# One place per weight chunk, and one region for early and late attention buffers, in a kernel of attention, low-rank mixing and a feed-forward

## The chip, the cores and the metric

The kernel runs on one core of a Trainium2 chip. The metric is the time of one execution on the device, in microseconds (us); of several executions the median is taken. Inside the core, TensorE (PE in the profile) multiplies matrices into PSUM, VectorE (DVE), ScalarE (ACT) and GpSimd (POOL) work on tiles, and SyncE (SP) issues the transfers between HBM and SBUF, all on one queue, in order.

## The reference

The inputs are `q`, `k`, `v` of 8 batches x 8 heads x 576 positions x 64, and the weights `U` (576x32), `V` (32x576), `w_ch1` (512x2048), `w_ch2` (2048x512). Cut to what matters:

```python
q_d, k_d, v_d = means of 4 neighbouring positions of q, k, v      # 144 positions
out_up    = repeat(softmax(q_d @ k_d.T / 8) @ v_d, 4)             # global part
out_local = softmax(where(|i - j| < 4, q @ k.T / 8, -1e9)) @ v    # band of 7 keys
x  = (out_up + out_local), heads side by side                     # 8 x 576 x 512
u  = x + (x.T @ U @ V).T                                          # mixing over positions
out = u + relu(u @ w_ch1) @ w_ch2                                 # feed-forward
```

The weights arrive in 64-bit floats.

## The kernel before

**Work.** Attention goes by head pairs: 4 pairs per batch, 32 in all, numbered here from 0. Pairs 0 to 3 (batch 0, "early", line 939) keep everything on the chip: `early_global`, `local_blocks`, `early_mix`. Pairs 4 and up ("late", line 951) go through DRAM: `late_global` stores the scores `s_s` and the global result `up_s`, `local_attn` reads them back (`sc`, `ul`), forms the products `Pt` on POOL (L800), sums them on DVE (L805) and stores `x_s`, and `mix_part` reads `x_s`, multiplies with `U` (`Ust`, L849) and `V` (`Vst`, L864), and leaves the feed-forward's input `u` as a high part `uH` and a rest `uL`. The early mixing does the same with L675, L677 and L692 to L695.

The feed-forward goes by steps (batch, half of 288 positions, chunk `fc` of 128 hidden units): 16 x 16 = 256 steps, 32 to a batch. `ffn1` (L889) does 12 matmuls into `ps_h`, ACT makes `hH` (L897), DVE `hL` (L898), and three steps later `ffn2` (L913) does 12 matmuls into the four banks `acc0` to `acc3`. A batch's first step needs `uH` and `uL` of all four pairs of that batch.

**Weights.** Each of the 32 chunks (16 of W1, 16 of W2) is loaded as raw 64-bit words, 512 KB, and converted (`convert`): ACT L343, DVE L345, L347, L349 with an intermediate `y` in a PSUM bank, ACT L354 writes the high part, POOL L357 the rest. W1 goes into two big tiles `W1H` and `W1L`. The raw words of W1, of the first three W2 chunks and of `U` pass through a ring of three buffers that they share with the late pairs' products:

```python
def raw_buf(name):
    return buf(loc, [128, 2 * CN], I32, name, "Pt:raw", 3)
```

The other W2 chunks have a place each, into which the raw words are loaded too. These places (`w2p`) lie where the early pairs' buffers were, so nothing is written to them before the early pairs are done: that point is an operation that the code calls `late` (line 961). The raw words of `Ub` (another layout of `U`) and of the two halves of `V` pass one after the other through one buffer (`eraw`).

**PSUM.** The banks are `acc0` to `acc3`, `h0`, `h1` and a ring of two, `m`. A conversion's `y` lies in `acc2` and `acc3` in turn for W1, in `h1` for W2 and `U`. The first `ffn2` waits until all 16 W1 chunks have their high part, since it takes these banks.

**Order.** The program is written out ahead of time by a planner (`Plan.run`): every operation has an engine, an estimated duration and a priority (smaller goes first). The planner simulates the five queues with these estimates, and each engine then executes its list in that order. On the chip an instruction that must wait holds back all behind it on its engine; SP's transfers too. Priorities: pair n has 10 n to 10 n + 2, W1 chunk f has 20 + 2 f, W2 chunk f has 20 + f, `U` 38, a feed-forward matmul over 1000 (so PE takes it when nothing of attention is ready), its relu -10.

Of the kernel before, what the change touches and what calls it, by code (L numbers as in the profile page):

```python
# [51 lines left out]
class Plan:  # L52
# [147 lines left out]
def attn_mix_ffn_kernel(ctx: ExitStack, tc, q, kp, vp, qT, kT, v, U, Ub, V, w1, w2, mask, band, eye, ex, pool, vw, vn, ident, outT):  # L200
# [15 lines left out]
    LAG = 3  # L216
    W1S, W2P, W2S = 2, 20, 1
    W1A, AT, W1B, W1C = 5, 25, 1.6, 15
# [3 lines left out]
    pw = lambda prio: PW0 if prio < 10 else PWx  # L222
    W1P = 20
    W2D = 4
    H1 = NFC + LAG
# [13 lines left out]
    const = ctx.enter_context(tc.tile_pool(name="const", bufs=1))  # L239
    loc = ctx.enter_context(tc.tile_pool(name="loc", bufs=1))  # L240
    glo = ctx.enter_context(tc.tile_pool(name="glo", bufs=1))
    mix = ctx.enter_context(tc.tile_pool(name="mix", bufs=1))
    ffn = ctx.enter_context(tc.tile_pool(name="ffn", bufs=1))
# [26 lines left out]

    mask_sb = const.tile([128, NPOS, 7], F32, name="mask_sb")
    warm = const.tile([128, 1], F32, name="warm")
# [4 lines left out]
    Vst = const.tile([128, S], F32R, name="Vst")  # L277
    W1H = const.tile([128, NDC, DF], F32R, name="W1H")
    W1L = const.tile([128, NDC, DF], F32R, name="W1L")
    early = tc.tile_pool(name="early", bufs=1)  # L280
    early_pool = early.__enter__()

    class Late:
        pool = None

        def open(self):
            early.__exit__(None, None, None)
            self.pool = ctx.enter_context(tc.tile_pool(name="w2p", bufs=1))

        def tile(self, *args, **kw):  # L290
            return self.pool.tile(*args, **kw)

    w2p = Late()

# [37 lines left out]
    def convert(raw, pp, n, hi_out, lo_out, a, wkey, name, prio, gate=(), l0=0):  # L332
# [18 lines left out]
        own = lambda k: [wkey + k] if isinstance(wkey, str) else [(wkey, k)]  # L351
        if gate:
            done.append(plan.ops[-1])
        act(n, lambda: nc.scalar.activation(hi_out(), ta(), AF.Copy), [t, *gate], own("H"), prio)  # L354
        if lo_out is None:
# [4 lines left out]

    def early_raw(name):
        return buf(early_pool, [128, S], I32, name, "eraw", 1)

    def raw_buf(name):
        return buf(loc, [128, 2 * CN], I32, name, "Pt:raw", 3)

    def load_ublk(prio):
        raw = early_raw("ur")
# [3 lines left out]
        pu = psum(ps_m, "ps_p", "m:p", 2)  # L372
        u4 = lambda: pu()[:QH, :2 * R].rearrange("p (a r) -> p a r", a=2)
# [8 lines left out]
    def load_u(prio):  # L382
        raw = raw_buf("ur")
        dma(lambda raw=raw: nc.sync.dma_start(out=raw()[:MP, :2 * MJ * R], in_=U.bitcast(I32)),
            [], [raw], prio, 150)
        convert(raw, MP, MJ * R, lambda: Ust[:, :, 0:R], lambda: Ust[:, :, R:2 * R], MJ, "U", "cu", prio)

    def load_v(prio):
        hs = S // 2
        for c in range(2):  # L390
            raw = early_raw("vraw")

            dma(lambda raw=raw, c=c: nc.sync.dma_start(
                out=raw()[:, :2 * hs], in_=V.bitcast(I32)[:, c * S:(c + 1) * S]), [], [raw], prio)
            cs = slice(c * hs, (c + 1) * hs)
            convert(raw, 128, hs, lambda cs=cs: Vst[:, cs].unsqueeze(1),
                    lambda cs=cs: Vst[3 * R:4 * R, cs].unsqueeze(1), 1, f"V{c}", "cv", prio, l0=3 * R)

    def load_w1(f, prio):
        raw = raw_buf("w1r")  # L400
        dma(lambda: nc.sync.dma_start(
            out=raw(), in_=w1.bitcast(I32)[f],
        ), [], [raw], min(prio - W1A, W1B + W1C * f if f < 3 else prio), 525)
        fs = slice(f * 128, (f + 1) * 128)
        convert(raw, 128, CN, lambda: W1H[:, :, fs], lambda: W1L[:, :, fs], NDC, f"W1_{f}", "c1", prio)

    W2 = [buf(w2p, [128, 2, DM], F32R, f"W2_{f}", f"W2_{f}:w") for f in range(NFC)]

    done = []

    def load_w2(f, prio):
        ahead = f < 3
        raw = raw_buf("w2r") if ahead else buf(w2p, [128, 2 * CN], I32, "w2r", f"W2_{f}:raw")
        dma(lambda: nc.sync.dma_start(out=raw(), in_=w2.bitcast(I32)[f * 128:(f + 1) * 128, :]),
            [] if ahead else ["late"], [raw], prio, 525, after=done[f - W2D:f - W2D + 1] if f >= W2D else ())
        convert(raw, 128, CN, lambda: W2[f]()[:, 0:1, :], lambda: W2[f]()[:, 1:2, :], 1, W2[f], "c2", prio, ["late"])

# [345 lines left out]
    def local_attn(b, hp, up_s, x_s, s_s, prio):  # L763
# [6 lines left out]
        sb = ex = ms  # L770
        dve(63, lambda: nc.vector.scalar_tensor_tensor(ms(), sc(), 0.125, mask_sb, op0=ALU.mult, op1=ALU.add),  # L771
            [sc, "mask"], [ms], prio)
        dve(63, lambda: nc.vector.tensor_reduce(out=mx(), in_=ms(), axis=AX.X, op=ALU.max), [ms], [mx], prio)
# [105 lines left out]
    def ffn1(s, i):  # L879
        b, t, fc = s  # L880
        uH, uL = u_of(b, t)
        ps = psum(ps_h, "ps_h", f"h{i % 2 * (i >= H1):d}:f", 1)
        fs = slice(fc * 128, (fc + 1) * 128)

        def mm():
            n = 0
            for dc in range(NDC):
                for w, u in ((W1H, uH), (W1H, uL), (W1L, uH)):
                    nc.tensor.matmul(ps()[:, :TN], w[:, dc, fs], u()[:, dc, :],  # L889
                                     start=(n == 0), stop=(n == 3 * NDC - 1))  # L890
                    n += 1
        ur = [(uH, c) for c in range(NDC)] + [(uL, c) for c in range(NDC)]
        mm_op[i] = op(PE, PH, mm, ur + [f"W1_{fc}H", f"W1_{fc}L"] + ["late"] * (i >= 3), [ps], FILL + i,
                      [mm_op[i - 1]] if i >= H1 else ())
# [7 lines left out]
    def ffn2(s, i):  # L902
# [6 lines left out]
        for e in range(NDC):  # L909
            def mm(e=e):  # L910
                es = slice(e * 128, (e + 1) * 128)
                for n, (w, hx) in enumerate(((0, hH), (0, hL), (1, hH))):
                    nc.tensor.matmul(ac[e]()[:, :TN], W2[fc]()[:, w, es], hx(),  # L913
                                     start=(fc == 0 and n == 0), stop=(fc == NFC - 1 and n == 2))
            first = [f"W1_{f}H" for f in range(NFC)] * (i == 0)
            op(PE, PF, mm, [hH, hL, (W2[fc], "H"), (W2[fc], "L")] + first, [ac[e]], FILL + i + LAG - 0.5)
        if fc == NFC - 1:
            uH, uL = u_of(b, t)
            for e in range(NDC):
                if e == NDC - 1:  # L920
                    o1 = buf(loc, [128, TN], F32, "o1", "o1b", 1)
                else:
# [118 lines left out]
```

## Time and profile before

| | |
|---|---|
| three runs | 1035.8, 1030.01, 1033.21 us; median 1033.21 |
| profiled execution | 1031.25 us, of which the trace spans 1029.4 us |
| PE, DVE, ACT, POOL busy | 990.8, 504.4, 390.2, 550.6 us |
| mean granted clock of TensorE | 0.983 |
| HBM read, written | 87.89 MB, 30.86 MB |

"Busy" of PE counts a matmul from its start to its modelled end, and pipelined matmuls overlap. In the views below a line number is that of the kernel's code, "out<-in" are the names of its tiles, and times in a list are us from the start of the span.

### The profile page before, as it was taken

The page shows a single profiled execution, that of the slowest core. Times are in us where ns is not written, and L with a number is a line of the kernel's source. Part 1 is how long each engine was busy: PE and PEld are TensorE (multiplying, and loading weights), DVE is VectorE, ACT ScalarE, POOL GpSimd, SP SyncE. Part 2 cuts the span into 40 slices and gives each one's busy share as a digit, 9 for nine tenths or more (in the row PEclk, how much of TensorE's full clock was granted, in tenths as well). Part 3 has the DMA queues.
Part 4 walks back from the last instruction along what each step waited for, and adds up shares of the span by engine and source line. Part 5 has one row for each costly group of instructions (what it writes and reads, how often), then busy time and mean ns, then how long its engine had stood idle before and what let it go on. Part 6 is the DMA issues. An engine that isn't in the chain of part 4 may idle for free.

```text
span 1029.4 us, 26839 instructions
## 1 busy us (share of the span) xinstructions
PE 990.8 (96%) x10792; PEld 972.9 (95%) x10792; DVE 504.4 (49%) x1022; ACT 390.2 (38%) x1239; POOL 550.6 (53%) x580
## 2 busy tenths in 40 slices
PE   5888979989999999999999999999999999999998
PEld 4677979989999999999999999999999999999998
DVE  4778986544454447544454545445654424212111
ACT  3667643433334334443343442334443232111110
POOL 3545895783756656685665756457575605211010
PEclk8899999989999999999999999999999999999999
DMA  9748854573454546555544453556555231000000
GB/s 291 200 136 237 256 132 123 133 154 98 103 142 105 142 118 148 121 120 144 121 126 115 122 122 83 122 134 156 126 135 129 78 76 35 24 1 24 1 24 24
DMA packets 222452, 120.51 MB, mean 117 GB/s; under 512 B 174756, under 2 KB 198136, under 8 KB 222328
## 3 DMA queue, kind: packets, MB, share of 16 engines
q1 hardware_dynamic: 222328, 118.79, 46.0%
q8 instruction: 85, 1.39, 0.6%
q14 instruction: 39, 0.32, 0.1%
HBM read 87.89 MB, written 30.86 MB: 115 GB/s over the span
## 4 chain that ended last, share of the span: by engine, by line
PE 90%; DVE 3%; ACT 2%; DMA 2%; issue 1%; SPq 1%; POOL 0%; DVEq 0%; ACTq 0%
PE acc L913 38%; PE ps_h L889 38%; PE ps_a L563 3%; PE ps_b L720 2%; PE ps_hu L849 2%; PE ps_t L550 1%; PE ps_b L727 1%; PE ps_u L864 1%; PE ps_v L445 1%; DMA w2r<-in_W 1%; DVE ms L771 1%; DMA ul<-up_s 1%; PE ps_u L695 1%; DMA pool_sb<-in_pool 0%; PE ps_hu L675 0%
## 5 line engine op out<-in xcount | busy, mean ns | idle before, releaser
L913 PE MATMUL acc<-hH,W 128*128 128x288 f32 x2048 | 464.0, 299 | 0.1
L913 PEld LDWEIGHTS acc<-hH,W 128*128 128x128 f32 x2048 | 344.8, 188 | 1.6 <-POOL W L357 0.5
L889 PE MATMUL ps_h<-uH,W1H 128*128 128x288 f32 x1024 | 305.9, 299 | 11.1 <-DVE hL L898 11.1
L889 PE MATMUL ps_h<-uL,W1H 128*128 128x288 f32 x1024 | 304.2, 297 | 0.0
L898 DVE SCALAR_TENSOR_TENSOR hL<-ps_h,hH 128x288 fp32r<-128x288 f32 x256 | 116.7, 456 | 382.4 <-ACT hH L897 381.6
L889 PE MATMUL ps_h<-uH,W1L 128*128 128x288 f32 x1024 | 302.9, 296 | 0.0
L913 PE MATMUL acc<-hL,W 128*128 128x288 f32 x1024 | 301.9, 295 | 0.0
L800 POOL TENSOR_TENSOR Pt<-vl,at 128x896 f32<-128x896 f32 (+1 forms) x140 | 241.9, 1806 | 90.3 <-DVE acc L805 40.2
L897 ACT ACTIVATE hH<-ps_h 128x288 fp32r<-128x288 f32 x256 | 105.1, 411 | 432.1 <-PE ps_h L889 431.8
L889 PEld LDWEIGHTS ps_h<-uH,W1H 128*128 128x128 f32 x1024 | 194.3, 190 | 12.9 <-DVE hL L898 12.6
L889 PEld LDWEIGHTS ps_h<-uH,W1L 128*128 128x128 f32 x1024 | 194.7, 190 | 0.0
L889 PEld LDWEIGHTS ps_h<-uL,W1H 128*128 128x128 f32 x1024 | 194.4, 190 | 0.0
L913 PEld LDWEIGHTS acc<-hL,W 128*128 128x128 f32 x1024 | 192.7, 188 | 0.0
L805 DVE TENSOR_REDUCE acc<-Pt 128x128 f32<-128x1024 f32 (+1 forms) x140 | 151.1, 1105 | 6.7 <-ACT Pt L794 2.4
L841 POOL TENSOR_TENSOR xL<-xL,xH 116x640 fp32r<-116x640 f32 x28 | 44.0, 1572 | 96.5 <-ACT xH L840 83.5
L872 POOL TENSOR_TENSOR uL<-xT,uH 128x288 fp32r<-128x288 f32 x56 | 44.3, 816 | 84.5 <-ACT uH L870 84.4
L924 POOL TENSOR_TENSOR o<-uH,uL 128x288 f32<-128x288 f32 x64 | 49.8, 817 | 53.0 <-DMA out_t<-o 53.0
L521 POOL TENSOR_TENSOR vr<-vr 72x256 f32<-72x256 f32 x56 | 41.6, 743 | 41.7 <-DMA vr<-in_v 37.0
L745 ACT ACTIVATE se<-ps_b 96x114 f32<-96x114 f32 x112 | 40.0, 357 | 59.3 <-PE ps_b L720 37.8
L794 ACT ACTIVATE Pt<-ul 128x128 f32<-128x128 f32 (+1 forms) x140 | 50.3, 444 | 18.7 <-DVE acc L805 14.5
L536 ACT ACTIVATE E<-ps_b,nb 72x144 f32<-72x144 f32 x112 | 40.9, 372 | 0.6
L531 DVE TENSOR_REDUCE mx<-ps_b 72x2 f32<-72x288 f32 x56 | 23.4, 449 | 27.6 <-ACT se L745 27.6
(137 smaller groups left out, 986.4 us busy)
## 6 DMA issues: line engine op xcount, KB each, us to landing
vl<-in_vp SPq DMA_DIRECT2D x56, 240.0 KB
out_t<-o SPq DMA_DIRECT2D x64, 144.0 KB
w1r<-in_W SPq DMA_DIRECT2D x16, 512.0 KB
w2r<-in_W SPq DMA_DIRECT2D x16, 512.0 KB
gT<-in_kT SPq DMA_DIRECT2D x28, 291.0 KB
gq<-in_qT SPq DMA_DIRECT2D x28, 288.0 KB
vr<-in_v SPq DMA_DIRECT2D x56, 144.0 KB
up_s<-od SPq DMA_DIRECT2D x112, 72.0 KB
```

Of the source, the lines that this page charges most:

```text
L521: pool_tt(256, lambda x=x: nc.gpsimd.tensor_tensor(out=x()[:, :, 0:2, :], in0=x()[:, :, 0:2, :], in1=x()[:, :, 2:4, :], op=ALU.add), [x], ...
L536: act(SD, lambda a=a, hh=hh, nb=nb: nc.scalar.activation(Es[hh]()[:, a, :], pooled_view(ps[hh])[:, a], AF.Exp, bias=nb()[:, a:a + 1], scal ...
L794: act(n * D, lambda n=n, ps=ps, Pt=Pt: nc.scalar.activation(Pt()[:, :n, :, 7], ul()[:, ps, :], AF.Copy), [ul], [(Pt, 1)], prio, 0.16)
L800: nc.gpsimd.tensor_tensor(out=Pt()[:, :n, :, 0:7].rearrange("p s d o -> p o s d"), in0=win, in1=at()[:, ps, :].rearrange("p s o -> p o s") ...
L805: dve(8.5 * n * D, lambda n=n, ps=ps, Pt=Pt: nc.vector.tensor_reduce(out=acc()[:, ps, :], in_=Pt()[:, :n], axis=AX.X, op=ALU.add), [(Pt, 0 ...
L841: pool_tt(640, lambda: nc.gpsimd.tensor_tensor(out=xL(), in0=xL().bitcast(F32), in1=xH().bitcast(F32), op=ALU.subtract), [xL, xH], [xL], prio)
L872: pool_tt(TN, lambda uH=uH, uL=uL, uf=uf: nc.gpsimd.tensor_tensor(out=uL()[:, hp, :], in0=uf(), in1=uH()[:, hp, :].bitcast(F32), op=ALU.su ...
L889: nc.tensor.matmul(ps()[:, :TN], w[:, dc, fs], u()[:, dc, :], start=(n == 0), stop=(n == 3 * NDC - 1))
L897: last_h[i] = act(TN, lambda: nc.scalar.activation(hH(), ps()[:, :TN], AF.Relu), [ps], [hH], FIRST, 0.05)
L898: dve(TN, lambda: nc.vector.scalar_tensor_tensor(hL(), ps()[:, :TN], 0.0, hH().bitcast(F32), op0=ALU.max, op1=ALU.subtract), [ps, hH], [hL ...
L913: nc.tensor.matmul(ac[e]()[:, :TN], W2[fc]()[:, w, es], hx(), start=(fc == 0 and n == 0), stop=(fc == NFC - 1 and n == 2))
L924: pool_tt(TN, lambda e=e, o1=o1: nc.gpsimd.tensor_tensor(out=o1()[:, :TN], in0=uH()[:, e, :].bitcast(F32), in1=uL()[:, e, :].bitcast(F32), ...
```

## The change

Each of the 32 weight chunks gets a place of its own (`wts`), for both parts, and its raw words are loaded into the same place; there is no ring for raw words any more. `Ub`, the two halves of `V` and `U` are loaded through the places of W2 chunks 15, 14, 13 and 12. The late pairs' three pools (`loc`, `glo`, `mix`) now lie where the early pairs' buffers were, and every operation that uses them comes after `late` (the `gate`). The conversions are in one list in order of use: W1 0 to 3, then W1 and W2 in turn, with priorities 30 to 45; a load is planned at the earliest when the conversion four places ahead of it is done. From the 13th conversion on `y` lies in `h1`, and the first `ffn2` waits for the first 12 chunks of the list. The early mixing's PSUM goes from the ring `m` to `acc0` and `acc1`. `U` has priority 36; the mask's load comes after `late`.

```diff
+        deps.update(d for k in (*r, *w) for d in getattr(getattr(k[0] if isinstance(k, tuple) else k, "pool", None), "gate", ()))
...
-    W1S, W2P, W2S = 2, 20, 1
+    W1F, WS = 4, 0.4
...
-    W1P = 20
-    W2D = 4
+    W1P = 30
+    WD = 4
+    NA = 12
...
-    W1H = const.tile([128, NDC, DF], F32R, name="W1H")
-    W1L = const.tile([128, NDC, DF], F32R, name="W1L")
...
+    loc, glo, mix = (Late(n) for n in ("loc", "glo", "mix"))
+
+    def open_late():
+        early.__exit__(None, None, None)
+        for p in (loc, glo, mix):
+            p.open()
...
-    dma(lambda: nc.sync.dma_start(out=mask_sb, in_=mask), [], ["mask"], 35, 32)
...
-        if gate or name == "cu" and lo_out is not None:
+        if own_bank:
             y = buf(ps_h, [128, CN], I32, "y_h", "h1:" + name, 1)
...
-    def early_raw(name):
-        return buf(early_pool, [128, S], I32, name, "eraw", 1)
-
-    def raw_buf(name):
-        return buf(loc, [128, 2 * CN], I32, name, "Pt:raw", 3)
+    def raw_in(f, name):
+        return buf(wts, [128, 2 * CN], I32, name, f"W2_{f}:{name}")
...
-            raw = early_raw("vraw")
+            raw = raw_in(NFC - 2 - c, "vraw")
...
+    W1 = [buf(wts, [128, 2, NDC, 128], F32R, f"W1_{f}", f"W1_{f}:w") for f in range(NFC)]
+    W2 = [buf(wts, [128, 2, DM], F32R, f"W2_{f}", f"W2_{f}:w") for f in range(NFC)]
+    weights, done = [], []
+
+    def load_w(w, src, hi, lo, a, prio, dprio):
+        weights.append(w)
+        raw = buf(wts, [128, 2 * CN], I32, "wr", w.tag + ":raw")
+        dma(lambda: nc.sync.dma_start(out=raw(), in_=src), [], [raw], dprio, 525,
+            after=done[len(done) - WD:len(done) - WD + 1] if len(done) >= WD else ())
+        convert(raw, 128, CN, hi, lo, a, w, "c" + w.tag[1], prio, len(done) >= NA)
...
-        ph = psum(ps_m, "ps_hu", "m:x", 2)
+        ph = psum(ps_acc, "ps_hu", "acc0:x", 1)
...
-            pu = psum(ps_m, "ps_u", "m:x", 2)
+            pu = psum(ps_acc, "ps_u", f"acc{1 - t}:x", 1)
...
-                for w, u in ((W1H, uH), (W1H, uL), (W1L, uH)):
-                    nc.tensor.matmul(ps()[:, :TN], w[:, dc, fs], u()[:, dc, :],
+                for w, u in ((0, uH), (0, uL), (1, uH)):
+                    nc.tensor.matmul(ps()[:, :TN], W1[fc]()[:, w, dc, :], u()[:, dc, :],
...
-            first = [f"W1_{f}H" for f in range(NFC)] * (i == 0)
+            first = [(w, "H") for w in weights[:NA]] * (i == 0)
...
-    for f in range(NFC):
-        load_w1(f, W1P + W1S * f)
-    plan.op(DVE, 0.0, w2p.open, [], ["late"], 27, after=early_ops, lat=0.0)
-    for f in range(NFC):
-        load_w2(f, W2P + W2S * f)
-    load_u(38)
+    for c in range(NFC + W1F):
+        if c < NFC:
+            load_w1(c, W1P + WS * (2 * c - min(c, W1F)))
+        if c >= W1F:
+            load_w2(c - W1F, W1P + WS * (2 * c + 1 - W1F))
+    late = plan.op(DVE, 0.0, open_late, [], [], 27, after=early_ops, lat=0.0)
+    for p in (loc, glo, mix):
+        p.gate.append(late)
+    load_u(36)
+    mask_sb = buf(loc, [128, NPOS, 7], F32, "mask")
+    dma(lambda: nc.sync.dma_start(out=mask_sb(), in_=mask), [], [mask_sb], 40, 32)
```

More of the change, by code (lines that the diff above doesn't have):

```diff
@@ L283, in attn_mix_ffn_kernel, with __init__ @@
     class Late:
-        pool = None
+        def __init__(self, name):
+            self.name, self.pool, self.gate = name, None, []
         def open(self):
-            early.__exit__(None, None, None)
-            self.pool = ctx.enter_context(tc.tile_pool(name="w2p", bufs=1))
+            self.pool = ctx.enter_context(tc.tile_pool(name=self.name, bufs=1))
         def tile(self, *args, **kw):
             return self.pool.tile(*args, **kw)
-    w2p = Late()
+    loc, glo, mix = (Late(n) for n in ("loc", "glo", "mix"))
[3 more added lines that the diff above has]
+            p.open()
     band_sb = early_pool.tile([128, NS * KL], BF16, name="band_sb")
@@ L351, in convert @@
         own = lambda k: [wkey + k] if isinstance(wkey, str) else [(wkey, k)]
-        if gate:
+        if not isinstance(wkey, str):
             done.append(plan.ops[-1])
-        act(n, lambda: nc.scalar.activation(hi_out(), ta(), AF.Copy), [t, *gate], own("H"), prio)
+        act(n, lambda: nc.scalar.activation(hi_out(), ta(), AF.Copy), [t], own("H"), prio)
         if lo_out is None:
@@ L359, in convert @@
             [t, *own("H")], own("L"), prio)
-    def early_raw(name):
-        return buf(early_pool, [128, S], I32, name, "eraw", 1)
-    def raw_buf(name):
-        return buf(loc, [128, 2 * CN], I32, name, "Pt:raw", 3)
+    def raw_in(f, name):
+        return buf(wts, [128, 2 * CN], I32, name, f"W2_{f}:{name}")
     def load_ublk(prio):
-        raw = early_raw("ur")
+        raw = raw_in(NFC - 1, "ubr")
         dma(lambda raw=raw: nc.sync.dma_start(
@@ L371, in load_ublk @@
         convert(raw, 128, NS * R, lambda: Ublk[:, :, 0:R], None, NS, "Ub", "cu", prio)
-        pu = psum(ps_m, "ps_p", "m:p", 2)
+        pu = psum(ps_acc, "ps_p", "acc1:p", 1)
         u4 = lambda: pu()[:QH, :2 * R].rearrange("p (a r) -> p a r", a=2)
@@ L382, in load_u @@
     def load_u(prio):
-        raw = raw_buf("ur")
+        raw = raw_in(NFC - 4, "ur")
         dma(lambda raw=raw: nc.sync.dma_start(out=raw()[:MP, :2 * MJ * R], in_=U.bitcast(I32)),
             [], [raw], prio, 150)
-        convert(raw, MP, MJ * R, lambda: Ust[:, :, 0:R], lambda: Ust[:, :, R:2 * R], MJ, "U", "cu", prio)
+        convert(raw, MP, MJ * R, lambda: Ust[:, :, 0:R], lambda: Ust[:, :, R:2 * R], MJ, "U", "cu", prio, True)
     def load_v(prio):
@@ L397, in load_v @@
                     lambda cs=cs: Vst[3 * R:4 * R, cs].unsqueeze(1), 1, f"V{c}", "cv", prio, l0=3 * R)
-    def load_w1(f, prio):
[L400 to L409, printed above, removed]
-    def load_w2(f, prio):
[L412 to L416, printed above, removed]
+    W1 = [buf(wts, [128, 2, NDC, 128], F32R, f"W1_{f}", f"W1_{f}:w") for f in range(NFC)]
[7 more added lines that the diff above has]
+        convert(raw, 128, CN, hi, lo, a, w, "c" + w.tag[1], prio, len(done) >= NA)
+    def load_w1(f, prio):
+        load_w(W1[f], w1.bitcast(I32)[f], lambda: W1[f]()[:, 0], lambda: W1[f]()[:, 1], NDC, prio,
+               min(prio - W1A, W1B + W1C * f if f < 3 else prio))
+    def load_w2(f, prio):
+        load_w(W2[f], w2.bitcast(I32)[f * 128:(f + 1) * 128, :], lambda: W2[f]()[:, 0:1, :],
+               lambda: W2[f]()[:, 1:2, :], 1, prio, prio)
     def work(is_early, pool, shape, dt, name, tag=None, bufs=1):
@@ L770, in local_attn @@
         sb = ex = ms
-        dve(63, lambda: nc.vector.scalar_tensor_tensor(ms(), sc(), 0.125, mask_sb, op0=ALU.mult, op1=ALU.add),
-            [sc, "mask"], [ms], prio)
+        dve(63, lambda: nc.vector.scalar_tensor_tensor(ms(), sc(), 0.125, mask_sb(), op0=ALU.mult, op1=ALU.add),
+            [sc, mask_sb], [ms], prio)
         dve(63, lambda: nc.vector.tensor_reduce(out=mx(), in_=ms(), axis=AX.X, op=ALU.max), [ms], [mx], prio)
@@ L882, in ffn1 @@
         ps = psum(ps_h, "ps_h", f"h{i % 2 * (i >= H1):d}:f", 1)
-        fs = slice(fc * 128, (fc + 1) * 128)
         def mm():
@@ L892, in ffn1 @@
         ur = [(uH, c) for c in range(NDC)] + [(uL, c) for c in range(NDC)]
-        mm_op[i] = op(PE, PH, mm, ur + [f"W1_{fc}H", f"W1_{fc}L"] + ["late"] * (i >= 3), [ps], FILL + i,
+        mm_op[i] = op(PE, PH, mm, ur + [(W1[fc], "H"), (W1[fc], "L")], [ps], FILL + i,
                       [mm_op[i - 1]] if i >= H1 else ())
@@ L920, in ffn2 @@
                 if e == NDC - 1:
-                    o1 = buf(loc, [128, TN], F32, "o1", "o1b", 1)
+                    o1 = buf(ffn, [128, TN], F32, "o1", "o1b", 1)
                 else:
```

7 lines of the change are left out of this document (2 added, 5 removed).

## The prediction

> **What bounds the kernel now.** I read the 40 slices first, then busy time by stretches, then the chain that ended last, then who waits on the SP queue and on DVE.
>
> ```profile
> PE   5888979989999999999999999999999999999998
> PEclk8899999989999999999999999999999999999999
> ```
>
> ```profile
> 0.00:77.00 77.00, 55.87 (x950) 47.67 (x951) 48.29 (x109) 43.23 (x130) 36.52 (x56) 0.89 0.69 210
> 77.00:225.00 148.00, 134.00 (x1547) 130.15 (x1546) 108.18 (x202) 77.77 (x234) 107.84 (x107) 0.94 0.67 175
> 225.00:1029.40 804.40, 800.91 (x8299) 795.06 (x8298) 347.96 (x711) 269.23 (x876) 406.25 (x417) 1.00 0.41 98
> ```
>
> The columns are: stretch, length, busy time of PE, weight loads, DVE, ACT, POOL, then the granted clock, DMA share and GB/s. From 225 us on PE is idle for 804.40 - 800.91 = 3.5 us at full clock: nothing is left to win there, and whatever moves the beginning moves the end by as much. So the change is decided before 225 us. In the stretch of 77 to 225 us PE loses 148.00 - 134.00 = 14.0 us to idling and 134.00 x 0.06 = 8.0 us to a low clock, 22.0 in all. What separates the stages is in the chain:
>
> ```profile
> 51.75 0.47 DVE cv L349
> 52.24 0.44 ACT Vst L354
> ...
> 77.34 1.64 PE ps_h L889 x12
> ...
> 219.06 0.82 PE ps_u L864 x2
> 219.88 5.61 PE ps_h L889 x24
> ```
>
> At 77.3 the feed-forward of batch 0 starts: the end of the early pairs, which I call E. At 219.1 pair 7's last mixing product comes, and batch 1's feed-forward follows at once. So the attention of batch 1 (pairs 4 to 7) is what ends last before the saturated part. The feed-forward is only just ahead of it:
>
> ```profile
> 215.93 0.46 PE L849 MATMUL ps_hu<-xL,Ust 116*64 116x128 f32 x5
> 219.06 0.82 PE L864 MATMUL ps_u<-Vst,stk 128*128 128x288 f32 x2 [2.67 <-DVE stk L854]
> ```
>
> PE has nothing but pair 7 to do from about 216 on. To gain much, both must come earlier: batch 0's feed-forward and the attention of pairs 4 to 7.
>
> **Raw words in their own places.** No instruction is added: 32 loads and 32 conversions stay, 12 matmuls a step too. The tiles keep 128x128 weights and 128x512 writes, so each instruction costs what it did: 0, with nothing to cover. What goes is the wait for the ring:
>
> ```profile
> SPq L401 <- DVE c L349: 28.5, 12, 4.3
> ```
>
> SP stood 28.5 us for raw buffers, and with it everything queued behind. Those buffers came free at DVE's pace, so the first question is what DVE could have done:
>
> ```profile
> 8.00:36.00 28.00, 20.00 (x417) 16.98 (x418) 13.92 (x36) 14.01 (x51) 9.50 (x14) 0.88 0.85 274
> 36.00:77.00 41.00, 34.31 (x462) 29.61 (x461) 29.83 (x63) 27.53 (x78) 22.12 (x25) 0.88 0.58 172
> L347 DVE SCALAR_TENSOR_TENSOR y_a<-w1r,y_a 128x512 int32<-128x512 int32 x13 | 9.0, 692 | 0.3
> L345 DVE TENSOR_SCALAR y_a<-c 128x512 int32<-128x512 int32 x13 | 8.9, 686 | 2.1 <-ACT c L343 1.8
> L349 DVE SCALAR_TENSOR_TENSOR c<-w1r,y_a 128x512 int32<-128x512 int32 x13 | 8.8, 679 | 0.2
> ```
>
> One chunk takes DVE 0.69 + 0.69 + 0.68 = 2.06 us; 13 chunks are done by E, 19 are left for the attention of batch 1 to share DVE with. From 8 to 36 us DVE idles 14.1 us: room for 6 chunks. Bounds: 0 chunks (the waits were for transfers and for early results) to 6 more by E. I take 3, the middle, because DVE's idle is scattered between the early pairs' own results. That leaves 3 x 2.06 = **6.2 us** less on DVE in the way of pairs 4 to 7 (0 to 12.4). From the 13th conversion on the intermediate has one bank instead of two, for four chunks of W1 that had two. DVE works through a chunk in sequence anyway; what it could lose is the idle before L345, 2.1 / 13 = 0.16 us, once more for each: 0 to 0.6 us, and I take 0.
>
> **V in places of its own.** Before, the second half of V waits for the first's buffer:
>
> ```profile
> 15.52 0.33 SPq L393 DMA_DIRECT2D vraw<-in_V  x1
> ...
> 36.18 0.37 SPq L393 DMA_DIRECT2D vraw<-in_V  x1
> ```
>
> It is issued 20.7 us after the first, and `Vst` is complete at 52.7, on the chain above; all eight early mixing products stand behind it. After, both halves can be loaded before 20 us, and the mixing of pairs 0 and 1 moves into PE's gaps. PE bounds what that can bring: in 36 to 77 us it idles 6.7 us and loses 34.31 x 0.12 = 4.1 to the clock, 10.8 together. I take E **5 us** earlier, at 72.3 (0 to 10.8), about half, since PE's own work stays the same and only its gaps can be filled. Weight conversions also now rank behind pairs 0 to 2; that is in the 5. The mixing's PSUM moves to `acc0` and `acc1`, which the local scores use: these are a few short holds, so 0, at worst 2 us back.
>
> **The shared region.** Now nothing of pair 4 may be loaded before E. Its loads go out at E, and the nearest rows for the way from there to its scores are pair 0's:
>
> ```profile
> 1.65 0.43 SPq L580 DMA_DIRECT2D qt<-in_qT  x1
> ...
> 4.67 0.67 POOL L429 TENSOR_TENSOR gh<-qt 128x288 f32<-128x288 f32 x1 [1.39 <-DMA qt<-in_qT]
> ...
> 6.54 0.43 POOL L431 TENSOR_TENSOR smk<-gh 128x144 f32<-128x144 f32 x1
> ```
>
> From issue to the pooled key 6.97 - 1.65 = 5.3 us. Before, that was done at 35 to 54 us, beside other work, and the scores came right after E:
>
> ```profile
> 35.00 0.60 SPq L580 DMA_DIRECT2D gq<-in_qT  x1
> ...
> 78.91 0.33 PE L727 MATMUL ps_b<-smk,smq 64*32 64x144 f32 x6
> ```
>
> After: 72.3 + 5.3 = 77.6 against 78.9, so **1.3 us** earlier. With E unmoved it would be 82.6, 3.7 later; with E at 66.5, 7.1 earlier. The wait now sits on SP: weight loads are queued behind it, but 15 chunks or so are then in place. The mask moves behind E too, one issue of 0.4 us; its first reader comes 14.8 us after pair 4's scores, so 0. `U` is converted earlier; pair 4's mixing, which needs it, comes tens of us later: 0.
>
> **What holds DVE at 145 us.** The largest loss of the middle stretch is one instruction:
>
> ```profile
> 145.00:160.00 15.00, 9.16 (x64) 8.92 (x63) 12.24 (x16) 5.91 (x24) 8.71 (x13) 0.77 0.41 105
> 145.45 6.20 DVE ms L771
> L771 DVE SCALAR_TENSOR_TENSOR ms<-sc,mask_sb x28: 209/218/6281, 93.7 to 849.4; 128x63 f32<-128x63 f32 x28
> 145.02 2.33 POOL L924 TENSOR_TENSOR o<-uH,uL 128x288 f32<-128x288 f32 x3
> ...
> 151.12 0.44 POOL L523 TENSOR_TENSOR vs<-vr 72x128 f32<-72x128 f32 x1
> PE ps_h L889 <- DVE hL L898: 11.1, 7, 5.8
> ```
>
> Its median is 0.22 us; once it takes 6.28, just while POOL runs without a gap from 145.02 to 151.56. The relu's DVE half stands behind it, and PE behind that, for 5.8 us at the longest. In the new order it need not meet such a run, but POOL has as much to do (107.84 of 148 us): I take half of 6.28 - 0.22 = 6.1, **3.0 us** (0 to 6.1). The Trainium skill, SBUF — State Buffer, section "Who interferes with whom", says that a DVE instruction with two SBUF inputs, as this one has, is shut out by a GpSimd instruction that reads SBUF, for the whole of it. The rows agree; by that rule alone the block is no late load and would come back wherever POOL is backlogged, and the sum would be 1024. Had it been a late load, which the new order moves, it would go whole, and the sum would be 1018.
>
> **The start of the feed-forward.** From 77 to 100 us PE loses a little as well:
>
> ```profile
> 77.00:100.00 23.00, 19.12 (x311) 17.73 (x310) 18.46 (x38) 17.83 (x53) 11.65 (x13) 0.93 0.82 246
> L354 ACT ACTIVATE W<-c x16: 615/628/682, 89.1 to 140.7; 128x512 fp32r<-128x512 f32 x16
> ```
>
> PE idles 3.9 us here and loses 1.3 us to the clock. `ffn2` waits for the high part of 16 chunks of W1 and for its own of W2, the first of which is written at 89.1; after, it waits for 12 chunks in order of use, which by the count above are done by E. I take 4 of these 5.2 us. With E's 5, and half of what PE loses from 145 to 160 us (5.8 idle and 9.16 x 0.23 = 2.1 of clock), batch 0's feed-forward ends 5 + 4 + 4 = 13 us earlier, near 203. That is more than the attention gains below, so PE waits for pair 7 again, some us longer than now, and this part is not in the sum.
>
> **Sum.** Attention of batch 1: 1.3 + 6.2 + 3.0 = 10.5 us earlier, at 208.6, and the saturated part with it. Against the profiled execution's own 1031.25: 1031.25 - 10.5 = **1021**. That execution is 1.96 us (0.2%) below the median of the three runs, inside their spread; I add nothing.
>
> **Rivals.**
> PE as the bound: pairs 4 to 7 keep up and PE loses nothing between E and the saturated part. That gives 5 + 22.0 = 27 us, **1004**. For it: pairs 4 to 7 leave DVE and POOL idle for 40 of 148 us each. Against: four pairs must then be done 16 us sooner than I reckon.
> Nothing comes of it: V and the ring were hidden behind PE's own early work, E stays, pair 4 starts 3.7 later, and the chunks converted ahead give that back. **1031**. For it: PE is 84% busy from 36 to 77 us.
> Slower, by weight loads in the way of early loads: SP's ring wait was also a brake. In the stretch of 10 to 20 us the transfers were already full:
>
> ```profile
> 10.00:20.00 10.00, 7.29 (x146) 5.84 (x145) 5.31 (x15) 5.01 (x20) 4.28 (x6) 1.00 1.04 333
> ```
>
> A chunk is 0.524 MB, 1.6 us at 333 GB/s. Four chunks, as many as may be planned ahead, in front of pair 3's loads cost 6.3 us: E at 83.6, pair 4's scores at 88.9, 10.0 late: **1041**. It decides (0.5% slower) from E at 78.8 on if no more chunks are converted than now, and from 85.0 on with 3 more.
>
> **How the numbers follow.** Forecast 0.52; its own range by the bounds above, not all at an end together, is 1012 to 1027. PE as the bound 0.20, nothing 0.15, slower 0.13. A measurement of this kernel can tell about 0.5%, 5 us, from no change: the forecast and the first rival are faster, 0.72; the second is 0.15; the third 0.13. The range 1002 to 1036 takes in the first two rivals and leaves out most of the third.
>
> **What would show it.** In the profile after: no wait of SP for L349; both V loads before 20 us and `Vst` before 30; E near 72; 16 conversions by then and the last by about 125 (now 141); pair 4's scores 5 us after E; the step of batch 1 near 209; no long L771 between E and there. The prediction is wrong if E does not move, if the attention takes longer from E than now (142 us), or if PE idles after 225 us.

## The result, and the profile after

The changed kernel took **1044.26 us** (median; 1041.75 to 1046.29), the kernel before 1032.5 us (median of four): ratio **1.0128** (95% interval 1.0086 to 1.0171). It is 1.3% slower; the prediction said 1021 us and faster. The profiled execution spans 1044.5 us, before 1029.4.

In the 40 slices of the changed kernel the ninth (209 to 235 us) is new: PE has 2 there, before 8, and the granted clock 5, before 8 (tenths):

```profile
PE   6989789929999999999999999999999999999998
PEclk8899999959999999999999999999999999999999
```

Busy time by stretches, same columns as before:

```profile
0.00:77.00 77.00, 61.91 (x1005) 53.78 (x1006) 51.65 (x116) 46.06 (x137) 33.90 (x51) 0.89 0.68 217
77.00:225.00 148.00, 122.68 (x1457) 117.31 (x1455) 95.53 (x183) 72.19 (x219) 103.57 (x105) 0.94 0.62 165
225.00:1044.50 819.50, 810.57 (x8332) 803.43 (x8332) 351.27 (x724) 270.40 (x884) 411.70 (x425) 0.99 0.40 97
210.00:220.00 10.00, 2.68 (x104) 2.02 (x104) 3.37 (x8) 5.07 (x20) 4.37 (x4) 0.70 0.66 187
220.00:230.00 10.00, 1.59 (x10) 1.22 (x10) 5.09 (x9) 1.49 (x3) 7.43 (x8) 0.50 0.71 139
```

PE does 6.0 us more up to 77 us (61.91 against 55.87) and 11.3 us less from 77 to 225 (122.68 against 134.00). The hole is at its end: from 210 to 230 us PE works 4.3 of 20 us. What it waits for stands in the chain of work:

```profile
68.19 0.63 PE ps_u L693 x6
...
231.22 0.59 PE ps_u L862
...
234.53 2.99 PE ps_h L886 x12
```

The early pairs end (E) at 68.8 us, 8.5 earlier than before; pair 7's last mixing product comes at 231.2, 12.2 later. Between the two lie 162.4 us, before 141.7. Batch 0's feed-forward is done by about 210, and batch 1's cannot start.

### The profile page after: what moved, and what is told of

Read it like the earlier page. It is cut to its first block, busy times and chain, and to the rows that moved or that the text cites. A ratio compares the mean times of both kernels' runs of the same rounds, so it can differ in the third digit from the quotient of the medians.

```text
span 1044.5 us, 26859 instructions
## 1 busy us (share of the span) xinstructions
PE 995.2 (95%) x10792; PEld 974.5 (93%) x10792; DVE 498.5 (48%) x1022; ACT 388.6 (37%) x1239; POOL 549.2 (53%) x580
## 4 chain that ended last, share of the span: by engine, by line
PE 85%; DMA 4%; DVE 3%; POOL 2%; ACT 2%; SPq 2%; issue 1%; POOLq 0%; DVEq 0%; ACTq 0%
PE ps_h L886 36%; PE acc L910 36%; PE ps_a L561 3%; PE ps_b L718 2%; PE ps_hu L847 1%; PE ps_t L548 1%; PE ps_b L725 1%; DMA ul<-up_s 1%; PE ps_v L443 1%; DVE acc L803 1%; PE ps_u L862 1%; DMA wr<-in_W 1%; PE ps_a L496 1%; DMA xL<-x_s 1%; POOL Pt L798 1%
## 5 line engine op out<-in xcount | busy, mean ns | idle before, releaser
L886 PE MATMUL ps_h<-uH,W 128*128 128x288 f32 x2048 | 455.1, 297 | 6.5 <-DVE hL L895 6.5
L886 PEld LDWEIGHTS ps_h<-uH,W 128*128 128x128 f32 x2048 | 344.8, 189 | 8.5 <-DVE hL L895 8.1
L886 PE MATMUL ps_h<-uL,W 128*128 128x288 f32 x1024 | 303.4, 296 | 0.0
L886 PEld LDWEIGHTS ps_h<-uL,W 128*128 128x128 f32 x1024 | 193.6, 189 | 0.0
L358 POOL TENSOR_TENSOR W<-c,W 128x512 fp32r<-128x512 f32 x32 | 41.1, 1287 | 41.5 <-ACT W L355 38.7
L718 PE MATMUL ps_b<-gT,gq 64*32 64x38 f32 x2016 | 36.6, 204 | 0.0
L924 DVE TENSOR_TENSOR o<-acc,o 128x288 f32<-128x288 f32 x64 | 26.2, 449 | 21.4 <-PE acc L910 21.4
```

What stands on the lines that cost most here:

```text
L718: nc.tensor.matmul(ps[hh]()[c * QL:(c + 1) * QL, r * KL:(r + 1) * KL], qr()[o, n * QL:(n + 1) * QL], kr()[o, n * QL:n * QL + KL], start=Tr ...
L886: nc.tensor.matmul(ps()[:, :TN], W1[fc]()[:, w, dc, :], u()[:, dc, :], start=(n == 0), stop=(n == 3 * NDC - 1))
```

## The experiments

Line numbers and names are those of each kernel; "gate" is the rule that the late pairs' pools open only at E. I started with three theories: **G**, the gate takes away the work done ahead for pairs 4 and 5; **S**, the transfer queue stands at the gate and the conversions starve; **O**, the new order of conversions is worse. A fourth, **R**, came up on the way: the planner writes out another order after any edit, and orders differ in time.

All of them, with E and the start of pair 7's last mixing product (P7) in the trace of one execution, in us. Each ratio is against executions of before taken beside it; single executions of one version lie up to 14 us apart (gate_off 1019.9 to 1033.7), and the traced one can be the fastest or the slowest:

| run | median | ratio to before (95%) | E | P7 | span |
|---|---|---|---|---|---|
| before | 1032.5 | 1 | 77.3 | 219.1 | 1029.4 |
| changed | 1044.26 | 1.0128 (1.0086 to 1.0171) | 68.8 | 231.2 | 1044.5 |
| gate_alone | 1043.94 | 1.0126 (1.0078 to 1.0174) | 77.6 | 227.0 | 1039.8 |
| nudge_gate_alone | 1043.87 | 1.0138 (1.0087 to 1.0189) | 80.5 | 229.0 | 1041.0 |
| gate_off | 1025.77 | 0.9955 (0.9923 to 0.9988) | 69.8 | 210.2 | 1022.9 |
| gate_planned_late | 1035.1 | 1.0037 (1.0011 to 1.0064) | 67.7 | 219.6 | 1032.8 |
| order_as_before | 1038.03 | 1.0063 (1.0041 to 1.0086) | 73.7 | 223.8 | 1037.7 |
| global_operands_free | 1025.01 | 0.9951 (0.9927 to 0.9974) | 65.4 | 209.0 | 1022.7 |
| v_places_alone | 1035.81 | 1.0042 (1.0010 to 1.0075) | 85.4 | 228.9 | 1039.3 |
| mixing_psum_back | 1026.55 | 0.9968 (0.9943 to 0.9994) | 83.6 | 212.1 | 1025.0 |
| gate_off_rest_late | 1023.66 | 0.9932 (0.9904 to 0.9960) | 68.5 | 207.5 | 1020.6 |
| nudge_after | 1032.33 | 1.0028 (0.9997 to 1.0058) | 66.1 | 214.9 | 1027.0 |
| nudge2_after | 1030.56 | 1.0007 (0.9972 to 1.0042) | 73.8 | 221.2 | 1033.3 |
| nudge3_after | 1032.78 | 1.0012 (0.9989 to 1.0036) | 66.4 | 219.6 | 1029.9 |
| nudge_psum_back | 1041.72 | 1.0112 (1.0072 to 1.0151) | 83.4 | 225.4 | 1039.2 |
| nudge_before | 1033.45 | 1.0014 (0.9981 to 1.0046) | 77.4 | 220.9 | 1031.6 |
| nudge2_before | 1033.07 | 1.0022 (0.9995 to 1.0048) | 77.4 | 222.1 | 1032.6 |
| nudge_gate_off | 1025.34 | 0.9957 (0.9930 to 0.9984) | 69.9 | 208.6 | 1023.2 |
| nudge_global_free | 1025.75 | 0.9944 (0.9918 to 0.9970) | 67.1 | 208.7 | 1023.9 |
| nudge_best | 1021.68 | 0.9903 (0.9865 to 0.9941) | 70.1 | 206.1 | 1019.3 |

Read the columns P7 and span together: their difference is 810 to 815 us in every row. The time goes with P7, not with E (83.6 goes with 1026.55, 68.8 with 1044.26). P7 is not always what PE waits for, though: in the four rows in which `loc` and `glo` are both open (gate_off, gate_off_rest_late and their nudges) PE comes to it from other work, without a wait. In gate_off, where the timeline names no wait:

```profile
210.18 0.43 PE L864 MATMUL ps_u<-Vst,stk 128*128 128x288 f32 x2
```

**gate_alone.** The kernel before, with only the gate:

```diff
+    for p in (loc, glo, mix):
+        plan.gate[id(p)] = [late]
```

> The kernel before, with one thing added: every operation of pairs 4 and up that uses a late buffer is planned after the last early operation, as in the changed kernel; all memory stays as it was. Theory G (the gate takes away the work that pairs 4 and 5 did before E, the end of the early pairs, and the attention of batch 1 ends that much later): 1042 to 1048, with E unmoved near 77 and the first feed-forward step of batch 1 near 232 instead of 219.7. Theory O (the order of the weight conversions, not the gate, is what costs): 1029 to 1035, like before.

Measured 1043.94 us. In its timeline pair 4's key is pooled (`smk`) 10.7 us after E instead of 23.6 before it, and P7 is 7.9 later (the traced execution as a whole 10.4, and it is the fastest of the four):

```profile
88.35 0.42 POOL L432 TENSOR_TENSOR smk<-gh 128x144 f32<-128x144 f32 x1
89.38 0.33 PE L728 MATMUL ps_b<-smk,smq 64*32 64x144 f32 x6
227.01 0.82 PE L865 MATMUL ps_u<-Vst,stk 128*128 128x288 f32 x2 [1.05 <-DVE stk L855]
```

The gate by itself costs 12 us in the kernel before. G holds so far, though it had put the step after P7 near 232.

**gate_off.** The changed kernel, with places of their own for `loc` and `glo`; in exchange W2 chunks 6 to 15 lie under the early region, beside `mix`, and `U`, `Ub` and `V` pass through places of W1:

```diff
+    own = {n: ctx.enter_context(tc.tile_pool(name=n, bufs=1)) for n in ('loc', 'glo')}
-    W2 = [buf(wts, [128, 2, DM], F32R, ...
+    W2 = [buf(wts if f < 6 else w2l, [128, 2, DM], F32R, ...
```

> The changed kernel, but the pools loc and glo of the late pairs have a place of their own and no gate; in their stead the chunks 6 to 15 of W2 lie, with the pool mix, where the early buffers were, and their loads wait for E; U, V and Ub pass through places of W1. Order and priorities of the conversions are those of the changed kernel. G: E stays near 71, pair 4 has its loads before E as in the kernel before, batch 1 starts its feed-forward 8 to 20 earlier than before, near 205: 1012 to 1026. Theory S (the transfer queue stands at the gate and starves the conversions): ten weight loads still wait for E, so the conversions still end near 145 and the time stays at 1040 or above. O: 1040 or above.

1025.77 us: faster than both kernels. The last chunk is converted later than in the changed kernel (its last DVE instruction starts at 150.9 us, there at 145.8), so the end of the conversions is not what set the time, against S.

**gate_planned_late.** The planner is told that the gate opens no earlier than 71 us, so that it queues more in front of it:

```diff
-    late = plan.op(DVE, 0.0, open_late, [], [], 27, after=early_ops, lat=0.0)
+    late = plan.op(DVE, 0.0, open_late, [], [], 27, after=early_ops, lat=0.0, at=71.0)
```

> The changed kernel with one number: the planner is told that the gate opens at 71 us at the earliest, which is when it opens on the chip, so the transfers of the late pairs stand in the queue behind the weight loads that come before that time. S: the queue no longer stands 22 us at the mask's load, 16 or more chunks are converted by E instead of 12, the last conversion is 10 us earlier than 145, and the time falls to 1025 to 1034. G: the conversions get ahead, yet the attention of batch 1 starts at E as it did: 1040 to 1048.

1035.1 us, 9 less than the changed kernel. It looked like S, but SP still stands 18.8 us at the gate (21.8 in the changed kernel) and 10 chunks are converted by E, not 16; and the nudges below show that an edit without any meaning moves as much, so this run decides nothing.

**order_as_before.** The changed memory, with the order and priorities of conversions of before (`load_w1(f, 20 + 2 * f)`, then `load_w2(f, 20 + f)`, `NA = 16`):

> The changed kernel with the conversions in the order and with the priorities of before: all of W1 first (priority 20 + 2 f), then W2 (20 + f), and the first second-layer matmul waits for the 16 chunks of W1 again. O: 1028 to 1036. G: the gate stays, so 1038 to 1048, a few us better at most because pairs 4 and 5 meet other conversions. S: 1040 to 1048.

1038.03 us: in this one order not back at before, as G had it and O had not. The nudges below move the changed kernel by more than the 6 us between the two, so alone it does not rule out O.

**global_operands_free.** As gate_off, but only `glo` (the pooled operands) has a place of its own, and W2 chunks 12 to 15 lie under the early region; mask, `loc` and `mix` stay behind the gate.

> The changed kernel, but only the pool of the global operands (glo: the halves and sums of pooled queries, keys and values of pairs 4 to 7) keeps a place of its own; in exchange W2 chunks 12 to 15 lie under the early region. The mask, the local operands (loc: padded values, local scores and products) and the mixing's (mix) stay behind the end of the early pairs. Theory P (what the change lost is the pooling of pairs 4 and 5 done ahead, and that lives in glo): pair 4's scores by 80 us at the latest and pair 5's by 96, batch 1's feed-forward step at 214 to 222 us, 1025 to 1033 us. Rival L (the padded values and the mask, which still stand on the SP queue with the weight loads behind them, are the loss): SP still stands 10 us or more, pooling of pairs 4 and 5 comes early but the local products do not, step at 226 to 232, 1036 to 1044 us.

1025.01 us, as with both pools open. In its timeline pair 4's key is pooled at 46.9 us, its scores come before E, and P7 at 209:

```profile
46.90 0.43 POOL L431 TENSOR_TENSOR smk<-gh 128x144 f32<-128x144 f32 x1
60.81 0.33 PE L727 MATMUL ps_b<-smk,smq 64*32 64x144 f32 x6
208.99 0.82 PE L864 MATMUL ps_u<-Vst,stk 128*128 128x288 f32 x2 [1.04 <-DVE stk L854]
```

So of what the gate shuts out, the pooled operands matter; the padded values and the mask may wait. One thing changes beside them: in this version SP hardly stands at the gate any more (in the changed kernel 21.8 us, the mask's line L966):

```profile
SPq L968 <- PE ps_u L695: 0.8, 1, 0.8
```

That was rival L's wait. But it brought the conversions next to nothing: 10 chunks are done by E as in the changed kernel, and the last one's last DVE instruction starts at 142.7 us instead of 145.8, while pair 7's scores come 18 us earlier. L is unlikely by these numbers; no run opens `glo` and keeps the wait.

**v_places_alone.** The kernel before, with `Ub` and the two halves of `V` in three raw buffers instead of one (tags `eraw0` to `eraw2`):

> The kernel before, with one part of the change alone: U's blocks and the two halves of V are loaded into three buffers of their own instead of one, so none waits for another. The ring, the order of conversions and the pools stay as before. My prediction's step (V in places of its own moves the end of the early pairs by 5 us): both V loads before 20 us, Vst before 30, end of the early pairs near 72 and about 5 us off the total, 1026 to 1028 us. Rival Q (the early pairs' end is moved by weight conversions ranking behind pairs 0 to 2, since with the order of before it stood at 76.9 although V had its places): V is complete early, but the early pairs end at 76 to 78 us and the total is 1029 to 1034 us.

1035.81 us. In its timeline and chain both loads of V go out at 6.1 us, and E is not earlier but at 85.4:

```profile
6.13 0.91 SPq L393 DMA_DIRECT2D vraw<-in_V  x2
```

```profile
84.83 0.61 PE ps_u L695 x6
```

In this order V's places bring E no gain; both theories missed that it would move back by 8 us. The traced execution is the slowest of its ten (1041.13 us) and has a granted clock of 0.80 from 36 to 77 us, before 0.88, so a part of the 8 us may be the clock's.

**mixing_psum_back.** The changed kernel, with the early mixing's PSUM in the ring `m` again:

```diff
-        ph = psum(ps_acc, "ps_hu", "acc0:x", 1)
+        ph = psum(ps_m, "ps_hu", "m:x", 2)
...
```

`ps_p` and `ps_u` go back to the ring likewise.

> The changed kernel, with the early mixing's PSUM (of the projections onto U's blocks and V) back in the two-buffer ring where it was before, instead of the two accumulator banks. My prediction priced this move at 0, at worst 2 us: the end of the early pairs at 71 +- 2 us, total 1042 to 1047 us. Rival B (the accumulator banks are what lets the mixing of pairs 0 to 3 run earlier): the end of the early pairs goes back to 75 to 78 us, and with it everything behind: 1047 to 1051 us.

Both theories missed: E goes back by 14.8 us to 83.6, but the time *falls* to 1026.55. Its waits of SP and its busy time between 71 and 83 us:

```profile
SPq L966 <- DVE stk L679: 32.2, 1, 32.2
```

```profile
71.00:83.00 12.00, 8.71 (x53) 7.60 (x53) 8.95 (x19) 7.36 (x25) 5.09 (x5) 0.72 0.00 0
```

SP stands 32.2 us at the gate and the DMA engines do nothing for the last 12 (share 0.00), more than in the changed kernel (19.0). A standing queue is thus not by itself the loss: the nudge of this version below stands as long (31.3 us) and takes 15 us more. Nor is the end of the conversions, whose last DVE instruction starts at 135.5 us here and at 136.0 in the nudge. S falls as the cause of the 12 us. But a kernel with the gate closed even longer at 1026 us also speaks against G. Hence theory R.

**gate_off_rest_late.** gate_off with the gate planned at 71 us or later (`at=71.0`):

> The version in which local and global operands have places of their own (W2 chunks 6 to 15 and the mixing's buffers lie under the early region), with one more edit: the planner takes the early region's end to be no earlier than 71 us, so that the ten gated W2 loads are queued behind what can go before. Theory S (a transfer queued behind a gate that opens later than planned costs what stands behind it): 4 to 6 us faster than without, 1020 to 1022 us, since loads of pair 4's and 5's later parts no longer stand behind gated W2 loads. Rival N (with pairs 4 and 5 free, nothing urgent stands behind the gated loads): 1024 to 1028 us, as without the edit.

1023.66 us, between the two expectations and 0.2% under gate_off by the ratios; with the nudge below the same edit gives 0.5%. So a small gain of S's kind is not excluded.

**The nudges.** One number of the planner's cost list is moved by 0.3%. Instructions, buffers and dependencies stay; the order in the queues changes:

```diff
-    PH, PF = 1.587, 0.398
+    PH, PF = 1.592, 0.398
```

> The changed kernel with one number of the planner's cost list moved by 0.3%: a feed-forward step is taken to last 1.592 us instead of 1.587. No instruction, buffer or dependency changes; only the order in which the queues are written out can. Theory G (the closed region itself costs the 12 us): 1040 to 1048 us, as without the nudge. Rival R (part of the loss is the accident of one written order, which a nudge deals anew): 1030 to 1039 us, with pair 7's last mixing product at 217 to 226 us instead of 231.

> The changed kernel with the early mixing's PSUM back in its ring (1026.55 us), and the same nudge of 0.3%. If the PSUM move was the cause of the loss: 1023 to 1030 us again. Rival R (its 18 us were a lucky order, since its early pairs end 15 us later than in the changed kernel and its gate stands closed even longer): 1035 to 1046 us, pair 7's last mixing product at 220 us or later.

> The kernel before with the same nudge of 0.3%. Theory G: within 5 us of before, 1026 to 1036 us. Rival R in its strong form (any order may come out 10 us off, and before was a lucky one): 1037 us or more.

> The version in which the local and global operands have places of their own (1025.77 us), with the same nudge of 0.3%. Theory G (with these two pools open early there is slack, so order matters little): 1021 to 1030 us. Rival R in its strong form: anything from 1018 to 1040 us, so above 1032 speaks for it.

The changed kernel fell to 1032.33 us, mixing_psum_back rose to 1041.72; before and gate_off stayed (1033.45 and 1025.34). P7 in the timelines of nudge_after, mixing_psum_back and nudge_psum_back:

```profile
214.94 0.82 PE L862 MATMUL ps_u<-Vst,stk 128*128 128x288 f32 x2 [1.04 <-DVE stk L852]
```

```profile
212.14 0.50 PE L862 MATMUL ps_u<-Vst,stk 128*128 128x288 f32 x2 [1.04 <-DVE stk L852]
```

```profile
225.41 0.82 PE L862 MATMUL ps_u<-Vst,stk 128*128 128x288 f32 x2 [1.04 <-DVE stk L852]
```

More orders: 1.582 instead of 1.587 (nudge2), a transfer rate of 289 instead of 290 (nudge3), and gate_alone nudged as above:

> The changed kernel with the feed-forward step taken as 1.582 us in the planner's list instead of 1.587 (the other way by 0.3%); nothing but the order of the queues can change. If the loss is a mean loss with a scatter of orders: 1030 to 1044 us, somewhere between the two orders seen (1032 and 1044). If the order of the change as made was one bad draw and the rest are level with before: 1027 to 1034 us.

> The changed kernel with the transfer rate in the planner's list taken as 289 instead of 290. The same two theories: mean loss with scatter, 1030 to 1044 us; one bad draw, 1027 to 1034 us. With the two orders known, three of four at 1034 or less would speak for the bad draw, three of four at 1035 or more for the loss.

> The kernel before with the feed-forward step taken as 1.582 us. Theory that open pools leave slack, so that orders matter little: 1027 to 1037 us, as the two orders known (1032 and 1033). If before scatters as much as the changed kernel: outside of that, up to 1042.

> The kernel before with the closed region alone (1043.94 us), and the feed-forward step taken as 1.592 us. If the closed region itself costs: 1038 to 1047 us again. If that was one bad order too: 1028 to 1036 us.

The changed kernel's four orders give 1044.26, 1032.33, 1030.56 and 1032.78 us. Three of four are level with before: the order of the change as made was a bad draw. gate_alone is 1043.87 again: there the 12 us are no accident of one order.

> The version with a place of its own for the global operands alone (1025.01 us), with the feed-forward step taken as 1.592 us. If the pooling ahead is what is won back, as the two orders of the version with both pools open suggest (1026 and 1025): 1021 to 1030 us, pair 7's last mixing product at 212 us or earlier. If it was a good order of a kernel that scatters like the changed one: 1031 to 1044 us.

> The version with both pools open and the region's end planned no earlier than 71 us (1023.66 us), with the same nudge. If open pools leave slack for any order: 1020 to 1028 us. If it was a good order: 1030 us or more.

1025.75 and **1021.68** us: the open pools keep their gain in a second order. Against the three level orders of the changed kernel, opening `glo` is worth 5 to 8 us; against the order as made, 19. In nudge_best, the fastest version (1.0% under before), PE idles 11.1 us from 77 to 225 us, at full clock:

```profile
77.00:225.00 148.00, 136.89 (x1596) 131.18 (x1595) 103.20 (x204) 77.63 (x233) 115.73 (x114) 1.00 0.70 181
```

## Why the prediction was wrong

**What held.** The bound. "So the attention of batch 1 (pairs 4 to 7) is what ends last" is so in before and in the changed kernel, where PE waits 2.7 us for P7's input at the last; the rest of the span after P7 is 810 to 815 us in all rows. It is no longer so where both pools are open, where PE comes to P7 without a wait. The prediction also named what would refute it, "if the attention takes longer from E than now (142 us)", and it took 162.4.

**The step that failed: "The shared region",** priced at 1.3 us of gain. Alone it costs 12 us in two orders. Its price was made at one place, pair 4's scores, as 5.3 us from the gate on. After the gate opens, SP, then POOL, show in their timelines:

```profile
68.87 0.33 SPq L966 DMA_DIRECT2D mask<-in_mask  x1
69.24 0.43 SPq L578 DMA_DIRECT2D gq<-in_qT  x1
69.72 0.43 SPq L578 DMA_DIRECT2D gT<-in_kT  x1
```

```profile
69.85 1.28 POOL L358 TENSOR_TENSOR W<-c,W 128x512 fp32r<-128x512 f32 x1 [1.08 <-ACT W L355]
72.77 1.30 POOL L358 TENSOR_TENSOR W<-c,W 128x512 fp32r<-128x512 f32 x1 [1.64 <-ACT W L355]
74.02 0.67 POOL L427 TENSOR_TENSOR gh<-gq 128x288 f32<-128x288 f32 x1
74.77 0.43 POOL L429 TENSOR_TENSOR smq<-gh 128x144 f32<-128x144 f32 x1
75.38 1.30 POOL L358 TENSOR_TENSOR W<-c,W 128x512 fp32r<-128x512 f32 x1 [0.18 <-ACT W L355]
76.63 0.68 POOL L427 TENSOR_TENSOR gh<-gT 128x288 f32<-128x288 f32 x1
77.26 0.74 POOL L519 TENSOR_TENSOR vr<-vr 72x256 f32<-72x256 f32 x1
77.96 1.30 POOL L358 TENSOR_TENSOR W<-c,W 128x512 fp32r<-128x512 f32 x1
79.22 0.43 POOL L429 TENSOR_TENSOR smk<-gh 128x144 f32<-128x144 f32 x1
```

From `gq`'s issue to the pooled key it is 79.65 - 69.24 = 10.4 us, twice the 5.3. The 5.3 came from pair 0 at the start of the span, when POOL had nothing else; here four conversions' rests (5.2 us in all) and a pooling of `vr` take turns with it. That error is only 5 us, and E came 3.5 earlier than forecast, so that pair 4's scores, at 80.4, lay near the predicted 77.6 in part by luck. The larger error is that the sum stopped there. Start of the pairs' scores, of pair 7's local softmax, and P7, from the timelines, in us:

| | pair 4's key pooled | scores 4 | 5 | 6 | 7 | softmax 7 | P7 |
|---|---|---|---|---|---|---|---|
| before | 53.7 | 78.9 | 93.2 | 119.6 | 143.3 | 168.9 | 219.1 |
| gate_alone | 88.4 | 89.4 | 105.7 | 132.9 | 162.0 | 181.9 | 227.0 |
| changed | 79.2 | 80.4 | 94.3 | 125.6 | 161.4 | 184.6 | 231.2 |
| nudge_after | 76.5 | 77.7 | 91.6 | 122.6 | 155.3 | 174.6 | 214.9 |
| global_operands_free | 46.9 | 60.8 | 81.5 | 114.6 | 143.0 | 166.4 | 209.0 |

The changed kernel is level with before at the scores of pairs 4 and 5 (1.5 and 1.2 us later), 6.0 behind at pair 6's and 18.1 at pair 7's. Before, SP and POOL did the loads and the pooling for pair 4 ahead, in gaps of the early pairs; now all of it is paid after the gate. Between E and P7 POOL has 10.5 us more to do than before (the first line is the changed kernel, the second before; POOL is the fifth of the busy times):

```profile
68.80:231.20 162.40, 131.44 (x1519) 125.47 (x1518) 106.70 (x205) 79.08 (x234) 113.81 (x117) 0.93 0.63 165
77.30:219.10 141.80, 127.80 (x1520) 123.95 (x1519) 102.79 (x191) 76.04 (x228) 103.35 (x100) 0.96 0.68 176
```

But no engine is full there (POOL 113.8 of 162.4 us): the time is lost in waits along the chain, and how the 10 us of work become 18 at pair 7's scores is not shown step by step. With `glo` alone open again, pair 4's scores are 20 us earlier than in the changed kernel and pair 7's 18.

**What is no step at all.** The gate costs 12 us, and yet three of the changed kernel's four orders are level with before: if the prices add, which was not shown, the rest of the change gives about 12 us back in them. Which part does was not separated (V alone and the order of conversions were tried in one order each). In the order as made nothing comes back. Changed kernel and nudge_after have the same instructions. The distance grows in the table: 2.7 us at pair 4's scores, 6.1 at pair 7's, 10.0 at its softmax, 14.7 at the store of its `x_s` (213.6 and 198.9 us), 16.3 at P7. These are the slowest execution of the one and the fastest of the other; the medians lie 11.9 apart. I took the planner's order as given. In four orders the change came out at +1.3%, +0.3%, +0.1% and +0.1%; neither my sum nor its range had a term for that. Why the changed kernel and mixing_psum_back scatter (1030.56 to 1044.26, 1026.55 to 1041.72) and before and the versions with `glo` open do not (each within 2.0 us) stays open. That work done ahead leaves slack for any order would fit, and where both pools are open PE indeed does not wait at P7; but it does in before and in global_operands_free, it was not tested by itself, and gate_alone, equal in its two orders, does not fit it.

**The other steps.** *Raw words in their own places:* the ring's wait went, but 10 chunks were converted by E (forecast 16; 13 before), and the last at 146.5 us (forecast 125; 140.7 before). Before had 10 done by 68.8 us as well: the pace did not change. The wait was replaced by one at the gate, as the step on the shared region said:

```profile
SPq L966 <- DVE stk L679: 19.0, 1, 19.0
...
SPq L966 <- PE ps_u L693: 2.8, 1, 2.8
```

From 47 to 68.9 us nothing was issued, but 15 chunks had been, as predicted, and mixing_psum_back shows that such a wait need not cost. The gain of 6.2 us was not there. (The one bank from the 13th conversion on met eight chunks of W1, not four; that bound was 1.3 us, not 0.6.) *V in places of its own:* E came 8.5 us earlier instead of 5, but nothing shows this to be the reason: V alone, in its one order, moved E back by 8. The accumulator banks for the early mixing, which I priced at "0, at worst 2 us back", moved E by 10 to 17 us: 83.4 and 83.6 with the ring, 66.1 to 73.8 with the banks. *What holds DVE at 145 us:* no long instruction of this kind between E and P7 (longest 1.29 us), as hoped, and it came to nothing since pair 7 was late anyway. *The start of the feed-forward:* batch 0's was done at 208.5, before 215.8, forecast near 203; it was not in the sum, and PE then waited for pair 7, as that step said. *The rivals:* three of the four orders lie where the second one, "Nothing comes of it", put them, at 1031 us, if by another balance. Slower came by another mechanism than the rival on that side: early loads were not held up (E at 68.8, not 83.6).

## What to carry to other kernels

Before memory is shared between an early and a late stage, list what the late stage does ahead of time in the early one's gaps, price it at the load that the engines will have afterwards, and follow it to the last consumer of the chain, not to the first. When queues are written out by a planner, time two or three meaningless nudges of its cost list for both kernels: a difference that a nudge removes belongs to the order, not to the change. Give back places to the operands that are worked on ahead (here the pooled operands, against the places of four weight chunks) before those that are only loaded ahead.

## What the runs showed of the hardware

The long DVE instruction came back later in the changed kernel, at 460 us, while POOL ran three products without a gap (timeline):

```profile
459.86 5.72 POOL L798 TENSOR_TENSOR Pt<-vl,at 128x896 f32<-128x896 f32 x3
460.65 4.84 DVE L769 SCALAR_TENSOR_TENSOR ms<-sc,mask 128x63 f32<-128x63 f32 x1
```

Its median is 0.22 us. The Trainium skill, SBUF — State Buffer, section "Who interferes with whom", has a DVE instruction with two SBUF inputs contend with a GpSimd instruction that reads SBUF, for the whole of that instruction. The trace agrees on the pair, but one product takes about 1.9 us (5.72 / 3), and the DVE instruction lasted 4.84: over the rest of a run of three, not of one.
